# Retention attention and a gated MLP on one core: every engine in emission order, weights staged in buffers of later pairs, units between the attention pieces

## The chip, the core and the metric

The kernel runs on one core of a Trainium2 chip. A core has a matrix engine (TensorE, PE in the profile; PEld is its loading of weights), VectorE (DVE), ScalarE (ACT), GpSimd (POOL) and SyncE (SP), which only issues transfers here. Each engine takes its own instructions from its own queue in order; semaphores make one wait for another. TensorE writes to PSUM, a small accumulator memory of eight banks, from which VectorE and ScalarE read. Transfers between the off-chip memory and the on-chip SBUF run on 16 DMA engines and are issued from SyncE's, ScalarE's or GpSimd's queue. The metric is the device time of one execution in microseconds.

## The reference

Eight batches of 576 positions, eight heads of 64. The attention has no softmax: scores are scaled, multiplied by a decay that depends on the distance and on the head, and causal. Its result, with the heads side by side as 512 columns, is `x` of a gated MLP whose gate mixes positions within a batch.

```python
scores = scale * np.matmul(q, k.transpose(0, 1, 3, 2))
gamma = 1.0 - 2.0 ** (-5.0 - np.arange(H, dtype=np.float32))
Dmat = np.where(rel >= 0, gamma[:, None, None] ** rel[None, :, :], 0.0)
x = np.matmul(scores * Dmat, v)              # to (B, S, 512)
h = x @ w_in                                 # (.., 1024), then tanh-gelu
u, v = h[..., :512], h[..., 512:]
v_n = (v - mean(v)) / sqrt(var(v) + 1e-06) * g_ln
v_s = np.einsum('ts,bsd->btd', w_sg, v_n) + b_sg[None, :, None]
out = x + (u * v_s) @ w_out
```

Inputs and output are float32; the kernel computes its products in bfloat16.

## The kernel before

Two batches make a pair of 1152 positions, cut into nine tiles of 128 (NT = 9, MID = 4: tile 4 has the last 64 positions of one batch and the first 64 of the next). Four pairs make N = 36 tiles, numbered through. For tile i the pieces are:

- `load(i)`: q, k and v from memory, issued by SyncE, in runs of 64 floats; five buffers (pool `ld`).
- `prep(i)`, GpSimd: q and k to bfloat16 (`qkb`), v times the key's decay (`vsc`).
- `attn_T(i)`: eight transposes into `tp` (one PSUM buffer), copied to `qT` by VectorE and in two halves to `kbd` by ScalarE and VectorE. The three copies read one PSUM bank and are ordered one behind the other, as are the two of `zbd`.
- `attn_S(i)`: scores `sc`, masked by VectorE into `ret`. `attn_O(i)`: output `ot` from the running state `zbd` and from `ret`; VectorE multiplies by the decay table `ttab` into `xT`. `attn_Z(i)`: the state `zp`, copied in two halves to `zbd`.
- `mlp_V(i)`: product `hv`, gelu by ScalarE (`vg`), mean and variance by VectorE (`bst`, `mv`), three small steps of GpSimd (`rs`, `rs`, `nm`), and ScalarE's normalisation `vn`. `mlp_U(i)`: product `hu`, gelu into `uT`.

When a batch has all its `vn`, it gives units of work: four mixing units `mlp_W` (ten products `wp` with the transposed w_sg, `wT`, and two VectorE products into `gT`) and four or five output units `mlp_O` (eight products `op`, ScalarE's copy `ob`, and a store that ScalarE issues). Before, `release` and `flush` queue the units of a batch, and each turn of the main loop ends with two of them, `run(2)`. `hv`, `hu`, `wp` and `op` share three PSUM buffers (tag `d` of `psD`); a mixing unit takes two of them.

In front of the loop stand tables: masks, decays, rows of g_ln and b_sg (`build_rows`, `place_rows`), and the weights. w_in and w_out come through `ld` buffers that tile loads use too, and VectorE converts them; w_sg comes by GpSimd's converting transfers. `build_wT` makes `wT`, three pieces a turn from turn 3, through the buffer `tp` and VectorE.

TensorE, GpSimd and SyncE run in the order in which the code emits:

```python
    ctx.enter_context(tc.manual_schedule(engines={mybir.EngineType.PE, mybir.EngineType.Pool, mybir.EngineType.SP}))
```

VectorE's and ScalarE's instructions are ordered by a scheduler.

Of the kernel before, what the change touches and what calls it, by code (L numbers as in the profile page):

```python
# [11 lines left out]
F32 = mybir.dt.float32  # L12
# [7 lines left out]
def kernel(  # L20
# [24 lines left out]
    outf = out.rearrange("b s d -> (b s) d")  # L45

# [32 lines left out]
    row4 = consts.tile([4, 2, S], F32, name="row4")
    nc.scalar.dma_start(row4[:, 0, :F2], moe_g_ln.partition_broadcast(4))  # L80
    nc.scalar.dma_start(row4[:, 1, :], moe_b_sg.partition_broadcast(4))
    load(0)
    nc.scalar.dma_start(g_col[:], moe_g_ln.rearrange("(c p) -> p c", p=128))

# [4 lines left out]
    w_stage = []  # L89
    for half in (1, 0):  # L90
        for c in (0, 2):
            wst = ld.tile([128, 2, F2], F32, name="wst", tag="qk")
            nc.sync.dma_start(wst[:], moe_w_in.rearrange("(c p) f -> p c f", p=128)[:, c:c + 2, half * F2:(half + 1) * F2])
            w_stage.append((half, c, wst))
        load(1 if half else 2)

    def nonzero(ap, tmp):
        nc.vector.tensor_scalar(tmp, ap, 1e-20, None, op0=Alu.is_lt)  # L100
        nc.vector.scalar_tensor_tensor(tmp, ap, -1e-20, tmp, op0=Alu.is_gt, op1=Alu.mult)
        nc.vector.scalar_tensor_tensor(ap, tmp, 3e-20, ap, op0=Alu.mult, op1=Alu.add)

    g_tmp = consts.tile([128, KK], F32, name="g_tmp")
    nonzero(g_col[:], g_tmp[:])
    row4b = consts.tile([4, 2, S], BF, name="row4b")
    row_t = consts.tile([4, S], F32, name="row_t")
    sel_i = consts.tile([4, 1], I32, name="sel_i")
    nc.gpsimd.iota(sel_i[:], pattern=[[0, 1]], base=0, channel_multiplier=1)
    sel = consts.tile([4, 3], F32, name="sel")  # L110

    def build_rows():
        nonzero(row4[:, 0, :F2], row_t[:, :F2])
        nc.vector.reciprocal(row4[:, 0, :F2], row4[:, 0, :F2])
        nc.vector.tensor_copy(sel[:, 0:1], sel_i[:])
        nc.vector.tensor_scalar(sel[:, 1:2], sel[:, 0:1], 2.0, -1.0, op0=Alu.is_ge, op1=Alu.mult)
        nc.vector.scalar_tensor_tensor(sel[:, 2:3], sel[:, 1:2], -2.0, sel[:, 0:1], op0=Alu.mult, op1=Alu.subtract)
        for a, n in ((0, F2), (1, S)):
            nc.vector.tensor_copy(row4b[:, a, :n], row4[:, a, :n])
            nc.vector.scalar_tensor_tensor(row4b[:, a, :n], row4b[:, a, :n], sel[:, 1 + a:2 + a], row4[:, a, :n],  # L120
                                           op0=Alu.mult, op1=Alu.add)

    def place_rows():
        for t in vmid:
            nc.sync.dma_start(t[0][NB0:NB0 + 4, :], row4b[:, 0, :F2])
            nc.sync.dma_start(t[1][0:4, :], row4b[:, 0, :F2])
        nc.sync.dma_start(wT[0][SB - 1][NB0:NB0 + 4, :], row4b[:, 1, :])
        nc.sync.dma_start(wT[1][0][0:4, :], row4b[:, 1, :])

# [6 lines left out]
                            compare_op=Alu.is_ge, fill=0.0, base=0, channel_multiplier=-1)  # L136
    tri_mid = consts.tile([128, 128], BF, name="tri_mid")
    NB0 = S - 128 * MID
    nc.vector.tensor_copy(tri_mid[:], tri[:])
    nc.vector.memset(tri_mid[:NB0, NB0:], 0.0)  # L140

    pos_i = consts.tile([128, S], I32, name="pos_i")
    nc.gpsimd.iota(pos_i[:], pattern=[[1, S]], base=-ORG, channel_multiplier=0)
    pos_f = consts.tile([128, S], F32, name="pos_f")
    nc.vector.tensor_copy(pos_f[:], pos_i[:])
    srow_i = consts.tile([128, NT], I32, name="srow_i")
    nc.gpsimd.iota(srow_i[:], pattern=[[128, NT]], base=-ORG, channel_multiplier=1)
    srow = consts.tile([128, NT], F32, name="srow")
    nc.vector.tensor_copy(srow[:], srow_i[:])
    nc.vector.tensor_scalar(srow[:, MID + 1:], srow[:, MID + 1:], float(-S), None, op0=Alu.add)  # L150
    nc.vector.tensor_scalar(srow[NB0:, MID:MID + 1], srow[NB0:, MID:MID + 1], float(-S), None, op0=Alu.add)
# [4 lines left out]
    lg_col = consts.tile([128, KK], F32, name="lg_col")  # L156
    lsc = consts.tile([128, 1], F32, name="lsc")
    nc.vector.memset(lsc[:], math.log(1.0 / math.sqrt(D)))
    for h in range(H):
        nc.vector.memset(lg_col[(h % 2) * 64:(h % 2) * 64 + 64, h // 2:h // 2 + 1], lng[h])  # L160

    ttab = consts.tile([128, KK, 128 * SB], F32, name="ttab")

    def build_ttab():
        for kk in range(KK):
            nc.scalar.activation(ttab[:, kk, :S], pos_f[:], Act.Exp,
                                 scale=lg_col[:, kk:kk + 1], bias=lsc[:])
        nc.gpsimd.tensor_copy(ttab[:, :, S:], ttab[:, :, :128 * SB - S])

    mhalf = consts.tile([128, 1], F32, name="mhalf")  # L170
    nc.gpsimd.memset(mhalf[:], -0.5)

    NV, NK, NZ = 5, 2, 2
    vpads = [consts.tile([128, H * D], BF, name=f"vsc{i}") for i in range(NV)]
# [4 lines left out]
    vmid = [[consts.tile([128, F2], BF, name=f"vmid{i}{e}") for e in range(2)] for i in range(2)]  # L179
    for t in vmid:  # L180
        nc.gpsimd.memset(t[0][NB0:, :], 0.0)
        nc.gpsimd.memset(t[1][:NB0, :], 0.0)
    for t in kbds + zbds:
        nc.vector.memset(t[:], 0.0)
    nc.vector.memset(kmid[:NB0, :], 0.0)

    def load_wsg():
        nc.gpsimd.memset(wnat[:, :, 0:64], 0.0)
        nc.gpsimd.memset(wnat[:, :, 64 + S:], 0.0)
        for j in range(SB):  # L190
            n = min(128, S - 128 * j)
            nc.gpsimd.dma_start(wnat[:n, j, 64:64 + S], moe_w_sg[128 * j:128 * j + n, :])

    def load_wout():
        for c in (0, 2):
            wst = ld.tile([128, 2, F2], F32, name="wst", tag="qk")
            nc.sync.dma_start(wst[:], moe_w_out.rearrange("(c p) f -> p c f", p=128)[:, c:c + 2, :])
            for r in range(2):
                nc.vector.tensor_scalar(w_out[:, c + r, :], wst[:, r, :], g_col[:, c + r:c + r + 1], None, op0=Alu.mult)


    wT = [[consts.tile([128, S], BF, name=f"wT{e}_{j}") for j in range(SB)] for e in range(2)]

    def build_wT(e, j):
        c0 = (64 if e == 0 else 0) + 128 * j
        tp = psA.tile([128, S], BF, name="wtp", tag="tp")
# [3 lines left out]
        nc.vector.tensor_copy(wT[e][j][:], tp[:])  # L210
# [6 lines left out]
    def prep(i):  # L217
# [4 lines left out]
        vp = vpads[i % NV]  # L222
# [6 lines left out]
    def attn_T(i):  # L229
        s = st[i]  # L230
        tp = psA.tile([128, 2, KK, 128], BF, name="tp", tag="tp")
        for a in range(2):
            for kk in range(KK):
                nc.tensor.transpose(tp[:, a, kk, :], s["qkb"][:, a, kk * 128:(kk + 1) * 128], ident[:])  # L234
        qT = work.tile([128, KK, 128], BF, name="qT")
        nc.vector.tensor_copy(qT[:], tp[:, 0, :, :])  # L236
        kbd = kbds[i % NK]
        nc.scalar.activation(kbd[:64, :, 0, :], tp[:64, 1, :, :], Act.Copy)  # L238
        nc.vector.tensor_copy(kbd[64:, :, 1, :], tp[64:, 1, :, :])  # L239
        s["qT"], s["kbd"] = qT, kbd  # L240

    def attn_S(i):
        s = st[i]
        m = i % NT
        ret = work.tile([128, H, 128], BF, name="ret")
        msk = (tri_mid if m == MID else tri)
# [10 lines left out]
    def attn_O(i):  # L257
        s = st[i]
        p, m = divmod(i, NT)
        if m == 0:  # L260
            xTs[p] = pairp.tile([128, KK, NT * 128], BF, name="xT")
# [17 lines left out]
    def attn_Z(i):  # L279
        s = st[i]  # L280
        p, m = divmod(i, NT)
# [9 lines left out]
        zb = zbds[i % NZ]  # L291
        nc.vector.tensor_copy(zb[:64, :, 0:64], z[:64, :, 0:64])
        nc.scalar.activation(zb[64:, :, 64:], z[64:, :, 64:], Act.Copy)
# [3 lines left out]
    vns = {}  # L297

    def mlp_V(i):
# [6 lines left out]
        nc.scalar.activation(vg[:], hv[:], Act.Gelu_apprx_tanh)  # L306
        bst = work.tile([128, 6], F32, name="bst")
# [153 lines left out]
```

## Time and profile before

| | us |
|---|---|
| median of 3 runs | 276.59 |
| lowest, highest run | 276.05, 278.32 |
| profiled execution | 279.28 |
| its span, first to last instruction | 277.6 |

In the span TensorE is busy 226.5 us (82%), its weight loads 166.9 (60%), VectorE 184.9 (67%), ScalarE 130.3 (47%) and GpSimd 121.7 (44%). The transfers move 42.0 MB. These shares are averages over a start-up, a long middle and a short end that have different limits, so they name no bound by themselves. Matmuls are pipelined, so the distance from the start of one to the start of the next tells more than a duration. In lists in order of time a row has the start, the duration, the engine, the line, the operation, out<-in, shapes, a count, and in brackets how long the engine had been idle and what ended that.

### The profile page before, as it was taken

The numbers are of one execution on the slowest core, as the hardware profiler recorded it, in microseconds if no ns is written. First come the engines' busy times: TensorE is split into PE (matmuls) and PEld (weight loads), VectorE is DVE, ScalarE is ACT, GpSimd is POOL, SyncE is SP. The second block draws the span as 40 slices with busy tenths as digits, with TensorE's granted clock in tenths as the row PEclk, the third lists the DMA queues.
The fourth block names the chain that finished last, engine by engine and source line by source line (L and its number), as shares of the span: only waits on it lengthen the run. The fifth ranks groups of instructions, "written<-read, shape, count | busy, mean of one in ns | idle before, by whom it ended". The sixth has DMA issues, their size and how long they took to land.

```text
span 277.6 us, 6581 instructions
## 1 busy us (share of the span) xinstructions
PE 226.5 (82%) x2626; PEld 166.9 (60%) x2626; DVE 184.9 (67%) x400; ACT 130.3 (47%) x230; POOL 121.7 (44%) x208
## 2 busy tenths in 40 slices
PE   0138967767899789997999799969997999789894
PEld 0025745656676577665776676657675777566552
DVE  4996766645886687766866887657767876686230
ACT  1154514415344554664465445564454475544513
POOL 7069871243144465544444545446445444421100
PEclk9999989759999999999999999999999999999999
DMA  8999999599202899789958896765586022100315
GB/s 166 269 258 200 224 273 191 115 201 188 53 0 78 208 212 207 192 205 214 208 133 183 191 199 170 207 154 118 118 211 167 0 78 75 42 2 0 116 38 189
DMA packets 120606, 42.02 MB, mean 151 GB/s; under 512 B 113825, under 2 KB 114425, under 8 KB 120577
## 3 DMA queue, kind: packets, MB, share of 16 engines
q1 hardware_dynamic: 114192, 31.49, 54.3%
q10 hardware_dynamic: 5728, 9.46, 9.4%
q0 software_dynamic: 656, 0.66, 1.5%
q8 instruction: 20, 0.33, 0.5%
q14 instruction: 10, 0.07, 0.1%
HBM read 32.80 MB, written 9.44 MB: 152 GB/s over the span
## 4 chain that ended last, share of the span: by engine, by line
PE 40%; DVE 27%; ACT 12%; issue 7%; POOL 5%; DMA 4%; ACTq 3%; POOLq 0%; SPq 0%; DVEq 0%
PE wp L345 8%; PE hv L303 7%; PE hu L332 6%; DVE bst L308 5%; ACT vg L306 4%; DVE xT L276 4%; ACT ob L363 4%; PE op L357 4%; PE sc L251 4%; PE tp L234 3%; PE ot L268 2%; ACTq L364 2%; POOL rs L313 2%; DVE gT L350 2%; DVE kbd_169 L239 2%
## 5 line engine op out<-in xcount | busy, mean ns | idle before, releaser
L312 POOL TENSOR_SCALAR rs<-mv 128x1 f32<-128x1 f32 x36 | 8.0, 222 | 121.7 <-DVE mv L310 115.8
L253 DVE TENSOR_TENSOR ret<-sc,tri 128x512 bf16<-128x512 f32 x64 | 41.0, 681 | 10.9 <-PE sc L251 10.9
L322 ACT ACTIVATE vn<-vg,nm,rs 128x512 bf16<-128x512 f32 x32 | 26.0, 812 | 37.5 <-POOL nm L315 37.5
L332 PE MATMUL hu<-xT,w_in 128*128 128x128 bf16 x576 | 41.2, 229 | 0.6 <-ACT ob L363 0.6
L308 DVE BATCH_NORM_STATS2 bst<-vg 128x6 f32<-128x512 f32 x36 | 25.0, 694 | 23.3 <-ACT vg L306 22.7
L345 PEld LDWEIGHTS <-vn 128*128 128x128 bf16 x256 | 24.5, 97 | 25.4 <-issue 18.7
L306 ACT ACTIVATE vg<-hv 128x512 f32<-128x512 f32 x36 | 21.5, 597 | 37.3 <-PE hv L303 31.0
L303 PE MATMUL hv<-w_in,xT 128*128 128x512 bf16 x144 | 37.9, 387 | 1.3 <-DVE xT L276 1.3
L221 POOL CAST qkb<-qk 128x1024 bf16<-128x1024 f32 x36 | 37.7, 1046 | 0.9 <-DMA qk<-in_k_dram 0.8
L332 PEld LDWEIGHTS <-w_in 128*128 128x128 bf16 x576 | 36.8, 103 | 1.4 <-issue 0.8
L350 DVE TENSOR_TENSOR gT<-wp,uT 128x288 bf16<-128x288 f32 x64 | 26.1, 447 | 17.3 <-PE wp L345 17.3
L357 PE MATMUL op<-w_out,gT 128*128 128x512 bf16 x144 | 37.0, 379 | 0.0
L234 PE MATMUL tp<-ident,qkb 128*128 128x128 bf16 x288 | 24.1, 232 | 10.9 <-POOL qkb L221 7.8
L234 PEld LDWEIGHTS <-qkb 128*128 128x128 bf16 x288 | 20.6, 104 | 18.6 <-POOL qkb L221 8.1
L276 DVE TENSOR_TENSOR xT<-ot,ttab 128x512 bf16<-128x512 f32 x36 | 24.9, 690 | 6.6 <-PE ot L273 6.0
L363 ACT ACTIVATE ob<-op 128x512 f32<-128x512 f32 x36 | 21.4, 593 | 13.3 <-PE op L360 8.1
L335 ACT ACTIVATE uT<-hu 128x512 bf16<-128x512 f32 x36 | 21.2, 590 | 12.2 <-PE hu L332 12.2
L313 POOL TENSOR_TENSOR rs<-rs,mhalf 128x1 f32<-128x1 f32 x36 | 20.4, 567 | 3.0
L236 DVE COPY qT<-tp 128x512 bf16<-128x512 bf16 x36 | 15.0, 417 | 8.3 <-PE tp L234 8.1
L251 PE MATMUL sc<-qT,kbd_168 128*128 128x128 bf16 x144 | 11.6, 224 | 9.7 <-ACT kbd_168 L238 9.0
L303 PEld LDWEIGHTS <-xT 128*128 128x128 bf16 x144 | 12.6, 100 | 11.2 <-DVE xT L276 2.3
L357 PEld LDWEIGHTS <-gT 128*128 128x128 bf16 x144 | 12.5, 98 | 9.2 <-DVE gT L350 0.3
(130 smaller groups left out, 379.0 us busy)
## 6 DMA issues: line engine op xcount, KB each, us to landing
out_dram<-ob ACTq DMA_DIRECT2D x36, 256.0 KB, 2.0
qk<-in_q_dram SPq DMA_DIRECT2D x32, 256.0 KB, 3.9
qk<-in_k_dram SPq DMA_DIRECT2D x32, 256.0 KB, 4.9
vf<-in_v_dram SPq DMA_DIRECT2D x32, 256.0 KB, 4.7
wst<-in_moe_w_in_dram SPq DMA_DIRECT2D x4, 512.0 KB, 5.9
qk<-in_q_dram SPq DMA_DIRECT2D x8, 128.0 KB, 4.7
qk<-in_k_dram SPq DMA_DIRECT2D x8, 128.0 KB
vf<-in_v_dram SPq DMA_DIRECT2D x8, 128.0 KB, 4.3
```

The lines of the kernel that those rows point to most:

```text
L221: nc.gpsimd.tensor_copy(qkb[:], qk[:].rearrange("p a h d -> p a (h d)"))
L234: nc.tensor.transpose(tp[:, a, kk, :], s["qkb"][:, a, kk * 128:(kk + 1) * 128], ident[:])
L253: nc.vector.tensor_tensor(ret[:, 4 * j:4 * j + 4, :], sc[:], msk[:].unsqueeze(1).to_broadcast([128, 4, 128]), op=Alu.mult)
L276: nc.vector.tensor_tensor(xTs[p][:, :, 128 * m:128 * m + 128], ot[:], ttab[:, :, t0:t0 + 128], op=Alu.mult)
L303: nc.tensor.matmul(hv[:], xTs[p][:, kk, 128 * m:128 * m + 128], w_in[:, kk, F2:], start=(kk == 0), stop=(kk == KK - 1))
L306: nc.scalar.activation(vg[:], hv[:], Act.Gelu_apprx_tanh)
L308: nc.vector.bn_stats(bst[:], vg[:])
L332: nc.tensor.matmul(hu[:, c, :], w_in[:, kk, 128 * c:128 * c + 128], xTs[p][:, kk, 128 * m:128 * m + 128], start=(kk == 0), stop=(kk == KK ...
L345: nc.tensor.matmul(ps[half][:], vns[t0 + j][e][:, 128 * c:128 * c + 128], wT[e][j][:, half * HS:(half + 1) * HS], start=(j == 0), stop=(j ...
L350: nc.vector.tensor_tensor(gTs[p][:, c, col:col + HS], ps[half][:], uTs[p][:, c, col:col + HS], op=Alu.mult)
L357: nc.tensor.matmul(op[:], gTs[p][:, c, r], w_out[:, c, :], start=(c == 0), stop=False, skip_group_check=True)
L363: nc.scalar.activation(ob[:], op[:], Act.Copy)
```

## The change

- All five engines are put in emission order (`manual_schedule()` without a list, at the top of the kernel).
- The first tile is laid out by hand: tile 0's attention stands ahead of the tables that it doesn't need, tiles 1 and 2 are prepared between the conversions of w_in.
- Weights no longer use `ld` buffers. `stage` loads w_in, w_sg and w_out into buffers of `gT` and `uT` that later pairs use; SyncE issues all of them. ScalarE converts w_in and w_sg; VectorE scales w_out, at turn 4 ahead of that tile's masks.
- `wT` pieces go through `psD` buffers and ScalarE, one between two pieces of a turn, from turn 4.
- The rows of 1/g_ln are made from the column by four small transposes; VectorE places the rows by six copies in place of six transfers.
- `mlp_V` is split: `mlp_norm(i - 2)` opens a turn behind the scores, `mlp_stats` and `mlp_rstd` follow later. The units run one behind the scores and one behind the transposes. A batch's units are released at the start of the third turn after its last tile.
- In `attn_T` k is transposed ahead of q and ScalarE's half of `kbd` is copied first; in `attn_Z` ScalarE's half of `zbd` is first.

```diff
+    ctx.enter_context(tc.manual_schedule())
...
+    def stage(src, tag, shape):
+        st = pairp.tile(shape, F32, name="wst", tag=tag)
+        nc.sync.dma_start(st[:], src)
+        return st
+
+    load(0)
+    st_v = stage(w_in_r[:, :, F2:], "gT", [128, KK, F2])
+    load(1)
+    st_u = stage(w_in_r[:, :, :F2], "gT", [128, KK, F2])
...
+    def cast_w(dst, st):
+        for c in (0, 2):
+            nc.scalar.activation(dst[:, c:c + 2, :], st[:, c:c + 2, :], Act.Copy)
...
-        tp = psA.tile([128, S], BF, name="wtp", tag="tp")
+        tp = psD.tile([128, S], BF, name="wtp", tag="d")
...
-        nc.vector.tensor_copy(wT[e][j][:], tp[:])
+        nc.scalar.activation(wT[e][j][:], tp[:], Act.Copy)
...
-        for a in range(2):
+        for a in (1, 0):
...
-        nc.vector.tensor_copy(qT[:], tp[:, 0, :, :])
         kbd = kbds[i % NK]
         nc.scalar.activation(kbd[:64, :, 0, :], tp[:64, 1, :, :], Act.Copy)
+        nc.vector.tensor_copy(qT[:], tp[:, 0, :, :])
         nc.vector.tensor_copy(kbd[64:, :, 1, :], tp[64:, 1, :, :])
...
     prep(0)
     attn_T(0)
+    attn_S(0)
+    attn_O(0)
+    attn_Z(0)
+    late_tables()
+    build_rows()
+    cast_w(w_in[:, :, F2:], st_v)
+    load(2)
+    prep(1)
+    attn_T(1)
+    cast_w(w_in[:, :, :F2], st_u)
+    load(3)
+    prep(2)
+    load(4)
+    st_sg = load_wsg()
+    for i in range(1, N + 1):
+        if i >= 3 and (i - 3) in last:
+            wo += batch_work(last[i - 3])
         if i + 4 < N:
             load(i + 4)
+        if i == 1:
+            st_out = stage(w_out_r, "gT", [128, KK, DM])
         if i + 2 < N:
             prep(i + 2)
+        if i == 4:
+            for c in range(KK):
+                nc.vector.tensor_scalar(w_out[:, c, :], st_out[:, c, :], g_col[:, c:c + 1], None, op0=Alu.mult)
+        if i == 6:
+            place_rows()
         if i < N:
             attn_S(i)
+        if i >= 2:
+            mlp_norm(i - 2)
+        if i >= 4:
+            build_wT()
+        run()
+        mlp_V(i - 1)
+        if i >= 4:
+            build_wT()
         if i + 1 < N:
             attn_T(i + 1)
+        mlp_stats(i - 1)
+        if i >= 4:
+            build_wT()
+        run()
+        mlp_rstd(i - 1)
+        mlp_U(i - 1)
+        if i >= 4:
+            build_wT()
         if i < N:
             attn_O(i)
             attn_Z(i)
+        if i == 2:
+            build_rows2()
+        if i == 3:
+            cast_wsg(st_sg)
+    mlp_norm(N - 1)
+    run(len(wo))
+    wo += batch_work(B - 1)
+    run(len(wo))
```

What stands in the queues, at three places. ScalarE in a turn with two output units, before (from the gelu of `hv` to the next one; `ob` and its DMA are the copy and store of an output unit):

```order
L306 ACTIVATE vg<-hv 128x512
L238 ACTIVATE kbd_168<-tp 64x4x128
L335 ACTIVATE uT<-hu 128x4x128
L322 ACTIVATE vn<-vg,nm,rs 128x512
L293 ACTIVATE zbd_171<-zp 64x4x64
L363 ACTIVATE ob<-op 128x512
L364 DMA out_dram<-ob 128x512
L363 ACTIVATE ob<-op 128x512
L364 DMA out_dram<-ob 128x512
```

and after, the same turn from its normalisation on:

```order
L349 ACTIVATE vn<-vg,nm,rs 128x512
L390 ACTIVATE ob<-op 128x512
L391 DMA out_dram<-ob 128x512
L322 ACTIVATE vg<-hv 128x512
L254 ACTIVATE kbd_155<-tp 64x4x128
L390 ACTIVATE ob<-op 128x512
L391 DMA out_dram<-ob 128x512
L362 ACTIVATE uT<-hu 128x4x128
L308 ACTIVATE zbd_158<-zp 64x4x64
```

`vn`, now of the tile before, and one output copy with its DMA have moved ahead of `vg` and `kbd`. VectorE in a turn with two mixing units, before:

```order
L253 TENSOR_TENSOR ret<-sc,tri 128x512 x2
L308 BN_STATS bst<-vg 128x6
L236 COPY qT<-tp 128x512
L310 BN_AGGR mv<-bst 128x2
L276 TENSOR_TENSOR xT<-ot,ttab 128x4x128
L239 COPY kbd_168<-tp 64x4x128
L292 CAST zbd_171<-zp 64x4x64
L350 TENSOR_TENSOR gT<-wp,uT 128x288 x4
```

and after:

```order
L269 TENSOR_TENSOR ret<-sc,tri 128x512 x2
L377 TENSOR_TENSOR gT<-wp,uT 128x288 x2
L255 COPY qT<-tp 128x512
L256 COPY kbd_155<-tp 64x4x128
L327 BN_STATS bst<-vg 128x6
L377 TENSOR_TENSOR gT<-wp,uT 128x288 x2
L332 BN_AGGR mv<-bst 128x2
L292 TENSOR_TENSOR xT<-ot,ttab 128x4x128
L309 CAST zbd_158<-zp 64x4x64
```

The four `gT` products, which stood together at the end, are in two pairs; `bst` and `mv` now follow `qT` and `kbd` of the next tile. VectorE at the turn from tile 3 to tile 4, after the change (`w_out` is the scaling of the staged weight):

```order
L292 TENSOR_TENSOR xT<-ot,ttab 128x4x128
L309 CAST zbd_158<-zp 64x4x64
L436 TENSOR_SCALAR w_out<-wst,g_col 128x512 x4
L269 TENSOR_TENSOR ret<-sc,tri_mid 128x512 x2
L255 COPY qT<-tp 128x512
L256 COPY kbd_156<-tp 64x4x128
```

Before, the scaling stood a tile later, behind the masks of tile 5 and around `bst`; now it is ahead of the masks of tile 4.

245 lines of the change are left out of this document (110 added, 135 removed).

## The prediction

> **What bounds the kernel now.** I read the page first, then TensorE's order of time for the rhythm, then its waits and the DMA's stretches.
>
> ```profile
> span 277.6 us, 6581 instructions
> ...
> PE   0138967767899789997999799969997999789894
> ...
> PEclk9999989759999999999999999999999999999999
> ```
>
> There are two stages with different limits. In the first nine slices (62 us) TensorE is often idle and part of the time at half clock; from slice 11 on it is nearly full. Below, "tile i" begins with its score product (sc). The rows show the starts of tiles 7, 11, 12, 13, 14, 15 and 34, two mixing products (wp) that waited, and an output unit (op).
>
> ```profile
> 72.63 0.61 PE L251 MATMUL sc<-qT,kbd_169 128*128 128x128 bf16 x8
> ...
> 97.48 0.28 PE L345 MATMUL wp<-wT_0_191,vmid_174 128*128 128x288 bf16 x1 [1.43 <-DVE gT L350]
> ...
> 98.58 0.61 PE L251 MATMUL sc<-qT,kbd_169 128*128 128x128 bf16 x8
> ...
> 104.02 0.28 PE L345 MATMUL wp<-wT_0_191,vmid_174 128*128 128x288 bf16 x1 [0.38 <-DVE gT L350]
> ...
> 105.11 0.61 PE L251 MATMUL sc<-qT,kbd_168 128*128 128x128 bf16 x8
> ...
> 109.75 0.59 PE L357 MATMUL op<-w_out,gT 128*128 128x512 bf16 x2
> ...
> 110.83 0.61 PE L251 MATMUL sc<-qT,kbd_169 128*128 128x128 bf16 x8
> ...
> 116.46 0.61 PE L251 MATMUL sc<-qT,kbd_168 128*128 128x128 bf16 x8
> ...
> 121.09 0.65 PE L251 MATMUL sc<-qT,kbd_169 128*128 128x128 bf16 x8
> ...
> 244.93 0.61 PE L251 MATMUL sc<-qT,kbd_168 128*128 128x128 bf16 x8
> ```
>
> So there are three parts: 72.6 us up to tile 7; 244.93 - 72.63 = 172.3 us for the 27 tiles 7 to 33; 277.6 - 244.9 = 32.7 us to the end. In the middle a tile with two output units takes 5.63 us (110.83 to 116.46), one with a single unit 4.63 (116.46 to 121.09). An output unit is 1.08 us (109.75 to 110.83). A mixing unit is 10 products, of which nine take 98.58 - 97.48 = 1.10, so 1.22. A tile with two mixing units could thus take 5.63 + 2 x 0.14 = 5.9 us; tile 11 took 6.53, and its second unit waited:
>
> ```profile
> PE wp L345 <- DVE gT L350: 10.8, 12, 1.4
> ```
>
> (That row covers 72 to 245 us.) Two mixing units in a row need four of three PSUM buffers, so the second stands until VectorE has emptied the first. TensorE's floor for the six batches of units in tiles 7 to 33 (each two mixing and two output tiles, in three of them another tile with one unit): 6 x (2 x 5.9 + 2 x 5.6) + 3 x 4.6 = 152 us against 172.3. These 20 us are the most that another order of the same work can return there.
>
> **The change, part by part.** The sum is made against the profiled execution (279.28 us, span 277.6), 1.0% over the median of the runs (276.59); I scale at the end.
>
> *First tiles.* The columns that end the next three rows are granted clock, DMA share and GB/s.
>
> ```profile
> 0.00:20.00 20.00, 2.48 (x19) 1.77 (x20) 15.51 (x40) 5.82 (x14) 8.67 (x21) 1.00 0.99 232
> 20.00:40.00 20.00, 15.67 (x161) 11.32 (x160) 14.32 (x30) 7.76 (x13) 17.78 (x27) 0.99 1.17 224
> ...
> 102.00:108.00 6.00, 5.62 (x66) 4.38 (x67) 5.03 (x11) 2.32 (x6) 3.04 (x5) 1.00 1.01 220
> ...
> 5.64 1.04 POOL L221 CAST qkb<-qk 128x1024 bf16<-128x1024 f32 x1 [0.84 <-DMA qk<-in_k_dram]
> ...
> L166 ACT ACTIVATE ttab<-pos_f,lsc,lg_col 128x576 f32<-128x576 f32 x4 | 3.3, 857 | 9.5 <-DVE tri_mid L140 9.5
> ...
> L155 ACT ACTIVATE gv<-srow 128x9 f32<-128x9 f32 x8 | 0.9, 200 | 0.0
> ...
> 54.20 0.86 DVE L199 TENSOR_SCALAR w_out<-wst,g_col 128x512 bf16<-128x512 f32 x2
> ...
> 24.20 1.91 PE L303 MATMUL hv<-w_in,xT 128*128 128x512 bf16 x4
> ...
> 29.72 0.61 PE L251 MATMUL sc<-qT,kbd_168 128*128 128x128 bf16 x8
> ...
> 40.68 1.91 PE L332 MATMUL hu<-xT,w_in 128*128 128x128 bf16 x16
> ...
> 80.92 1.06 PE L332 MATMUL hu<-xT,w_in 128*128 128x128 bf16 x16
> ```
>
> When loads land: by 40 us the DMA has moved 20 us x (232 + 224) GB/s = 9.1 MB at full share. SyncE's new order has, up to the end of w_out, six tiles of 0.786 MB, w_in 2.1, w_sg 1.33 and w_out 1.05 MB, in all 9.2 MB, so w_out lands at about 40.4 us, and tiles 6, 7 and 8 0.786 MB / 0.215 = 3.7 us apart behind it (44, 48, 51.5). No entry of that queue waits for a buffer: w_out's needs ScalarE's first conversion of w_in, done by 16.
>
> The front gets quicker. Tile 0 is cast at 5.64 as before, then come transposes at half clock (1.0 us) and three copies of its PSUM buffer in series (0.58, 0.41, 0.43): its score product starts at 9.4, since the tables that took VectorE up to 15 us now stand behind it. Before tile 1, ScalarE converts half of w_in. No row shows such a conversion; from the ttab and gv rows 128x1024 is 0.2 + 1015 x (857 - 200)/567 ns = 1.4 us, with 0.86 (the shorter row) and 1.7 (twice it) as ends. From 12.9 two of them end at 15.7, the three copies at 17.1: tile 1. A tile without units is 5.63 - 2.16 = 3.5 us of products warm, up to twice that cold: tiles 2, 3, 4 at 23.5, 30 and 35. The second half of w_in is converted beside this, and if it weren't covered it would cost 2.8 us.
>
> Tile 4 stands: in VectorE's order the scaling of w_out is ahead of its masks (ret). They wait for 40.4 and four scalings (0.86 a pair), to 42.1, and end at 43.4. ScalarE converts w_sg meanwhile (five at 0.86, 35 to 39.4). TensorE, idle from 35.2 to 39.4, is at half clock then (hu x16 in 1.91 us at 40.68; 1.06 warm at 80.92), and wT, hv, wT, tp, wT, hu, wT and the output products last until 46.1. Tile 5 starts there. From its nm at 47 ScalarE has vn, wT, vg, wT and kbd (3.1 us, a wT taken as vg's 0.6), then VectorE two copies: tile 6 at 51. Tile 6 has two vmid of 0.81, wT, vg, wT and kbd from 53.3: tile 7 at **58** (before 72.6). Ends: 53, when only the landing of tile 7 (48) and its 5 us of cast, small steps and copies bind; 64, when DMA and chain each slip 3 us. The six rows that VectorE now copies, and their table, are some 3 us that lie under the waits for DMA; uncovered they would cost those 3 us.
>
> [...]
>
> *Middle.* The work of a tile stays the same; units move between the attention pieces, and the normalisation (vn) into the next tile's turn. With units apart the next hv and tp (1.3 us) cover VectorE's two gT products, so 5.9 us is reached where VectorE is on time. But the fixed order closes a ring through three engines, once per tile: ScalarE's vn, ob and its DMA issue, vg, kbd; VectorE's qT, kbd, bst, mv; GpSimd's three small steps; the next vn. qT now stands behind ScalarE's kbd, bst and mv behind qT. Before, bst and vn of a tile didn't wait for the next tile's copies. The ring's price from rows, start to start:
>
> ```profile
> 109.80 0.81 ACT L322 ACTIVATE vn<-vg,nm,rs 128x512 bf16<-128x512 f32 x1 [0.76 <-POOL nm L315]
> 110.52 0.58 ACT L363 ACTIVATE ob<-op 128x512 f32<-128x512 f32 x1
> ...
> 93.00 0.60 ACT L363 ACTIVATE ob<-op 128x512 f32<-128x512 f32 x1 [0.41 <-ACT ob L363]
> ...
> 94.02 0.60 ACT L306 ACTIVATE vg<-hv 128x512 f32<-128x512 f32 x1 [0.41 <-PE hu L332]
> 94.51 0.58 ACT L238 ACTIVATE kbd_169<-tp 64x512 bf16<-64x512 bf16 x1
> ...
> 107.86 0.41 DVE L236 COPY qT<-tp 128x512 bf16<-128x512 bf16 x1
> 108.19 0.17 DVE L310 BATCH_NORM_AGGREGATE mv<-bst 128x2 f32<-128x6 f32 x1
> ...
> 259.42 0.69 DVE L308 BATCH_NORM_STATS2 bst<-vg 128x6 f32<-128x512 f32 x1 [4.27 <-ACT vg L306]
> ...
> 260.22 0.18 DVE L310 BATCH_NORM_AGGREGATE mv<-bst 128x2 f32<-128x6 f32 x1
> ...
> 261.81 0.81 ACT L322 ACTIVATE vn<-vg,nm,rs 128x512 bf16<-128x512 f32 x1 [1.45 <-POOL nm L315]
> ```
>
> Output tile: vn to ob 0.72, ob to vg 1.02 (the DMA issue is in it), vg to kbd 0.49, kbd 0.58, qT 0.33, VectorE's kbd 0.40 (an estimate beside qT's pace), bst to mv 0.80, mv to vn 1.59: **5.93 us**, more than TensorE's 5.63. Mixing tile: no ob (less 1.02), bst's own 0.69 in place of 0.80, and two gT (0.82) ahead of mv: 5.6, less than TensorE's 5.9. So the ring binds output tiles once its slack is used up. After two mixing tiles vn starts 1.7 us into a tile (kbd ends at 3.8, qT, kbd, bst, gT until 6.0, 1.59, less 5.9). The next score product can't start before kbd is copied, 3.65 us after vn. The first output tile keeps 5.6 (vn slips to 2.0), the second takes 2.0 + 3.65 = 5.7, a third with one unit 5.9 to 6.0 in place of 4.6. Then vn is 2.3 us late and VectorE 1.8: unit one's gT end at 3.9 us in place of 2.7, unit two starts at 3.65 in place of 3.0, and this mixing tile takes 6.6, the next 5.9. Batches: 6.6 + 5.9 + 5.6 + 5.7 = 23.8, and 29.8 with the third output tile; three of each give **160.8 us** against 172.3. Ends: 152 with slack everywhere, 172 with nothing won.
>
> GpSimd's cast of tile i+2 is ahead of the small steps, so the DMA must be in time. A tile moves 0.786 in and 0.262 MB out: 4.8 us at 220 GB/s, under 5.9.
>
> *End.* The mixing of the batch before last now runs a tile later. From tile 34: 6.6 + 5.5 (no transposes) + 6.1 (hv, hu, four output units), then four mixing units, 1.22 + 3 x 1.68 (266.90 - 265.22), and the last outputs, 277.6 - 268.0 = 9.6, which don't change. Sum **34.1** against 32.7.
>
> ```profile
> 265.22 0.28 PE L345 MATMUL wp<-wT_0_191,vmid_176 128*128 128x288 bf16 x1 [0.30 <-DVE gT L350]
> ...
> 266.90 0.28 PE L345 MATMUL wp<-wT_0_191,vmid_176 128*128 128x288 bf16 x1 [0.30 <-DVE gT L350]
> ...
> 268.00 1.03 PE L357 MATMUL op<-w_out,gT 128*128 128x512 bf16 x4
> ...
> L364 ACTq DMA_DIRECT2D out_dram<-ob x36: 338/338/1042, 85.2 to 274.3; - x36
> ...
> DMA packets 120606, 42.02 MB, mean 151 GB/s; under 512 B 113825, under 2 KB 114425, under 8 KB 120577
> ```
>
> Span: 58.0 + 160.8 + 34.1 = 252.9, 24.7 less than before. Execution: 279.28 - 24.7 = 254.6; scaled by 276.59/279.28, **252 us**.
>
> **The rivals.** *The ring has slack and TensorE bounds the middle.* For: the same operations ran at 5.63 us a tile in another order, so no engine's own work is the bound. Against: the ring's rows follow each other by data or by queue and add to 5.93. The middle would be 152: 252.9 - 8.8 = 244.1, scaled 243.5; with tile 7 at 53, 238.5.
>
> *The middle wins nothing.* The ring at 6.4 us on each of 27 tiles makes 172.8; the front's 14.6 and the end's -1.4 remain: 264. For: a DMA issue of ScalarE has stood 1.04 us. Against: its median is 0.34.
>
> *Slower: loads arrive late.* GpSimd stands at the cast of tile i+2; the small steps, vn, kbd and the score product stand behind it. The gain is gone where a tile takes (160.8 + 24.7)/27 = 6.9 us, which is 1.05 MB at 152 GB/s; at 145 a tile takes 7.2 us and the kernel 286. Against: stretches at full share move 220 and more. The span's mean of 151 has idle DMA in it.
>
> That the change doesn't do what it says gets no chance: the built order has units apart and all engines as written.
>
> **How the numbers follow.** Forecast 0.74 (alone 245 to 260); ring with slack 0.12 (238 to 245); middle wins nothing 0.09 (260 to 272); late loads 0.05, of which 0.03 are slower and 0.02 about as before. Under 1% can't be told from no change (the runs spread by 0.8%). Faster by over 1%: 0.74 + 0.12 + 0.09 = 0.95; within 1%: 0.02; slower: 0.03. The range takes in parts of both neighbours: 242 to 264.
>
> **What would show it.** Tile 7's score product at 58; VectorE idle ahead of the scaling of w_out, ended by its DMA near 40; TensorE idle from about 35 to 39. In the middle, output tiles of 5.6 to 6.0 us, ScalarE's vn waiting for nm and VectorE's qT for ScalarE's kbd, a first mixing tile of 6.6. Wrong: 50 us for nine tiles (slack), a cast of GpSimd waiting for a load after 80 us (late loads), tile 7 past 64 (front).

## The result, and the profile after

The changed kernel takes 269.44 us (median of four runs, 266.47 to 270.21); the kernel before, on the same chip, took 276.75 (276.05 to 278.32). The ratio is 0.971, with a 95% interval of 0.962 to 0.979: faster by 3%, where 252 us was forecast and 242 to 264 given as the range. The profiled execution took 269.32 us. The head of the changed kernel's page:

```profile
span 267.6 us, 6555 instructions
...
PE   0558669868999999969999999799999999799894
...
PEclk9999986999999999999999999979999999889999
```

Over the first nine slices together TensorE is fuller than before. From there on it is full but for dents in slices 18, 26 and 35, and behind two of them, in slices 27 and 35 to 36, the granted clock dips. TensorE's order of time shows what stands there; these rows are starts of score products (sc) of tiles 7, 14, 15, 16, 25, 34 and 35, with the last products ahead of tile 16:

```profile
59.58 0.22 PE L267 MATMUL sc<-qT,kbd_156 128*128 128x128 bf16 x1
...
103.32 0.67 PE L267 MATMUL sc<-qT,kbd_155 128*128 128x128 bf16 x8
...
109.36 0.92 PE L267 MATMUL sc<-qT,kbd_156 128*128 128x128 bf16 x8
...
114.32 0.40 PE L305 MATMUL zp<-vsc_150,qkb 128*128 128x128 bf16 x4
116.36 0.22 PE L267 MATMUL sc<-qT,kbd_155 128*128 128x128 bf16 x1 [1.64 <-ACT uT L362]
...
173.16 0.22 PE L267 MATMUL sc<-qT,kbd_156 128*128 128x128 bf16 x1 [1.64 <-ACT uT L362]
...
231.09 0.22 PE L267 MATMUL sc<-qT,kbd_155 128*128 128x128 bf16 x1 [1.63 <-ACT uT L362]
...
239.49 0.61 PE L267 MATMUL sc<-qT,kbd_156 128*128 128x128 bf16 x8
```

- Front: tile 7 at 59.6 us, forecast 58.0, before 72.6. The gain is there.
- Middle, tiles 7 to 33: 231.09 - 59.58 = **171.5** us, forecast 160.8, before 172.3. Nothing is gained.
- End: 267.6 - 231.1 = 36.5, forecast 34.1, before 32.7.

So 10.7 of the 14.7 us by which the span of 252.9 was missed lie in the middle. There the output tile from 103.32 takes 6.04, and the one with a single unit 7.00 (109.36 to 116.36), in which TensorE stands for 1.64 us ahead of tile 16's score product. The row names uT of ScalarE, which is only the last semaphore seen; the engines' own order (below) shows qT written just then. The waits of the middle, grouped (waiting engine and line, what ended the wait, us in total, times, longest):

```profile
ACT vn L349 <- POOL nm L337: 35.3, 24, 2.5
DVE qT L255 <- ACT kbd_155 L254: 24.5, 14, 3.0
DVE qT L255 <- ACT kbd_156 L254: 20.8, 13, 3.0
...
PE sc L267 <- ACT uT L362: 4.9, 3, 1.6
```

ScalarE waits for GpSimd's nm ahead of every vn (24 times, and three more ahead of a vmid), VectorE for ScalarE's kbd ahead of every qT (27 of 27). That is the ring of the forecast. Its links, from the vn in tile 14's turn to the normalisations of the next two turns (ScalarE, VectorE and GpSimd in order of time):

```profile
105.82 0.82 ACT L349 ACTIVATE vn<-vg,nm,rs 128x512 bf16<-128x512 f32 x1 [1.46 <-POOL nm L337]
106.66 0.60 ACT L390 ACTIVATE ob<-op 128x512 f32<-128x512 f32 x1
107.28 0.34 ACTq L391 DMA_DIRECT2D out_dram<-ob  x1
107.67 0.60 ACT L322 ACTIVATE vg<-hv 128x512 f32<-128x512 f32 x1 [0.41 <-ACT ob L390]
108.16 0.58 ACT L254 ACTIVATE kbd_156<-tp 64x512 bf16<-64x512 bf16 x1
108.77 0.42 DVE L255 COPY qT<-tp 128x512 bf16<-128x512 bf16 x1 [2.15 <-ACT kbd_156 L254]
109.23 0.43 DVE L256 COPY kbd_156<-tp 64x512 bf16<-64x512 bf16 x1
109.69 0.69 DVE L327 BATCH_NORM_STATS2 bst<-vg 128x6 f32<-128x512 f32 x1
110.49 0.18 DVE L332 BATCH_NORM_AGGREGATE mv<-bst 128x2 f32<-128x6 f32 x1
112.10 0.81 ACT L346 ACTIVATE vmid_162<-vg,nm,rs 64x512 bf16<-64x512 f32 x1 [1.46 <-POOL nm L337]
112.93 0.81 ACT L346 ACTIVATE vmid_163<-vg,nm,rs 64x512 bf16<-64x512 f32 x1
113.76 0.60 ACT L390 ACTIVATE ob<-op 128x512 f32<-128x512 f32 x1
...
115.27 0.58 ACT L254 ACTIVATE kbd_155<-tp 64x512 bf16<-64x512 bf16 x1
...
115.88 0.42 DVE L255 COPY qT<-tp 128x512 bf16<-128x512 bf16 x1 [2.97 <-ACT kbd_155 L254]
...
119.21 0.81 ACT L349 ACTIVATE vn<-vg,nm,rs 128x512 bf16<-128x512 f32 x1 [2.48 <-POOL nm L337]
```

Start to start it is 0.84 (vn to ob), 1.01, 0.49, 0.61, 0.46, 0.46, 0.80 and 1.61: 6.28 us from 105.82 to 112.10, against 5.93 in the forecast. The next round takes 7.11 (to 119.21), because the tile over the batch border is normalised in two vmid of 0.83 each, and this falls in the very turn with a single output unit (15, 24 and 33). In that turn ScalarE's kbd ends at 115.85, qT at 116.30, and TensorE, done with zp at 114.72, stands until 116.36.

### The profile page after: what moved, and what is told of

The parts are those of the page before. It is cut to its first block, busy times and chain, and to the rows that moved or that the text cites. A ratio compares the mean times of both kernels' runs of the same rounds, so it can differ in the third digit from the quotient of the medians.

```text
span 267.6 us, 6555 instructions
## 1 busy us (share of the span) xinstructions
PE 227.5 (85%) x2594; PEld 164.6 (62%) x2630; DVE 176.4 (66%) x394; ACT 143.1 (53%) x249; POOL 117.6 (44%) x202
## 4 chain that ended last, share of the span: by engine, by line
PE 40%; DVE 19%; SPq 12%; ACT 10%; issue 8%; DMA 4%; POOL 4%; ACTq 2%; POOLq 0%; DVEq 0%
PE wp L372 13%; SPq L78 10%; PE hv L319 7%; PE hu L359 6%; DMA qk<-in_k_dram 4%; DVE bst L327 4%; DVE xT L292 3%; PE op L384 3%; ACT ob L390 3%; PE tp L251 3%; DVE qT L255 3%; DVE gT L377 3%; PE ot L284 2%; ACT kbd_155 L254 2%; ACT kbd_156 L254 2%
## 5 line engine op out<-in xcount | busy, mean ns | idle before, releaser
L255 DVE COPY qT<-tp 128x512 bf16<-128x512 bf16 x36 | 15.2, 424 | 60.0 <-ACT kbd_155 L254 35.3
L238 POOL CAST qkb<-qk 128x1024 bf16<-128x1024 f32 x36 | 37.4, 1038 | 21.3 <-DMA qk<-in_k_dram 17.1
L359 PE MATMUL hu<-xT,w_in 128*128 128x128 bf16 x576 | 39.4, 224 | 1.5 <-ACT wT_3_186 L227 1.5
L359 PEld LDWEIGHTS <-w_in 128*128 128x128 bf16 x576 | 35.5, 100 | 2.4 <-issue 1.6
L384 PE MATMUL op<-w_out,gT 128*128 128x512 bf16 x128 | 34.7, 379 | 0.8
L267 PE MATMUL sc<-qT,kbd_156 128*128 128x128 bf16 x144 | 13.0, 225 | 5.7 <-ACT uT L362 2.4
```

The source lines that it names most:

```text
L238: nc.gpsimd.tensor_copy(qkb[:], qk[:].rearrange("p a h d -> p a (h d)"))
L359: nc.tensor.matmul(hu[:, c, :], w_in[:, kk, 128 * c:128 * c + 128], xTs[p][:, kk, 128 * m:128 * m + 128], start=(kk == 0), stop=(kk == KK ...
L384: nc.tensor.matmul(op[:], gTs[p][:, c, r], w_out[:, c, :], start=(c == 0), stop=False, skip_group_check=True)
```

## The experiments

The theory: **the closed ring through ScalarE, VectorE and GpSimd sets the middle.** Against it stand: the loads, VectorE's own queue, and ScalarE's load as such (its work, not the closing of a loop). Each ratio below is to the kernel before, run on the same chip in the same session (medians of 278.4 to 279.6 us); the changed kernel's is 0.971 (0.962 to 0.979).

**Open the ring at vn.**

```diff
         attn_S(i)
-        if i >= 2:
-            mlp_norm(i - 2)
...
             attn_T(i + 1)
+        if i >= 2:
+            mlp_norm(i - 2)
```

> ScalarE's normalisation (vn) of tile i-2 is emitted behind the copies of tile i+1's transposes, and so behind kbd, in place of ahead of the first unit. Everything else is the changed kernel. Ring theory (vn, ob, vg, kbd, qT, kbd, bst, mv, vn, 6.29 us per output tile in the changed kernel, sets the middle): vn no longer delays kbd, the loop is open, TensorE bounds the tiles: mixing 5.9, output 5.6, one-unit output about 4.6 to 5; the four waits of a first score product (1.6 us each) and the two half-clock stretches behind them go. Tiles 7 to 33 take 152 to 157 us in place of 171.5, the kernel 249 to 255 in place of 269. Rival 'loads': the DMA sets the pace, and the time stays within 2 us of 269. Rival 'VectorE': its queue (gT twice, ret, xT in a fixed order) sets the mixing tiles: those stay at 7.2, only the output tiles shorten, 263 or more.

Measured: 249.6 us, ratio 0.894 (0.886 to 0.901). The middle took 157.1 us (59.94 to 217.01) in the profiled execution, which was the longest of the four (253.3 us). TensorE's score products of tiles 15 and 16, and ScalarE around one vn:

```profile
108.50 0.61 PE L267 MATMUL sc<-qT,kbd 128*128 128x128 bf16 x8
...
113.13 0.72 PE L267 MATMUL sc<-qT,kbd 128*128 128x128 bf16 x8
```

```profile
106.02 0.58 ACT L254 ACTIVATE kbd<-tp 64x512 bf16<-64x512 bf16 x1
106.49 0.81 ACT L349 ACTIVATE vn<-vg,nm,rs 128x512 bf16<-128x512 f32 x1
```

The one-unit tile takes 4.63 in place of 7.00 and has no wait; vn starts with no wait of its own, behind kbd. No instruction was added or taken away, so neither the loads nor ScalarE's or VectorE's work can be what the changed kernel's middle stood for.

**Open it at another link.**

```diff
         mlp_V(i - 1)
+        mlp_stats(i - 1)
+        mlp_rstd(i - 1)
...
-        mlp_stats(i - 1)
...
-        mlp_rstd(i - 1)
```

> VectorE's bst and mv of tile i-1, and GpSimd's three steps behind them, are emitted right behind hv, ahead of tile i+1's transposes and copies; vn stays ahead of vg and kbd. Ring theory: the loop is now vn, ob, vg, bst, mv, vn: 0.84 + 1.01 + 0.6 + 0.8 + 1.62 = 4.9 us, less than TensorE's 5.6, and no longer goes through kbd and qT; qT and the next score product stand 0.5 us later behind vg than before, which the slack takes. Middle 153 to 159, kernel 250 to 257: about as much as with vn moved. If instead it is only vn's place ahead of kbd that counts (ScalarE's load, not a closed loop), this edit gives nothing or loses: 268 to 272.

Measured: 249.3 us, ratio 0.894 (0.887 to 0.902), the middle 156.0 us (56.97 to 212.99). VectorE's order, with mv ahead of the copies:

```profile
107.67 0.69 DVE L327 BATCH_NORM_STATS2 bst<-vg 128x6 f32<-128x512 f32 x1 [1.74 <-ACT vg L322]
108.47 0.18 DVE L332 BATCH_NORM_AGGREGATE mv<-bst 128x2 f32<-128x6 f32 x1
108.57 0.39 DVE L255 COPY qT<-tp 128x512 bf16<-128x512 bf16 x1
108.99 0.43 DVE L256 COPY kbd<-tp 64x512 bf16<-64x512 bf16 x1
```

Here vn stays ahead of kbd and the gain is the same. The loop that is left (vn, ob, vg, bst, mv, vn) is shorter than TensorE's tile by the estimate above, 4.9 against 5.6 us. Two edits at different engines, each of which takes links out of the ring, return 14.4 and 15.5 us of the middle: it is the closed loop, and not the place of vn.

**Shorten one link.** The stores go to SyncE's queue.

```diff
-        nc.scalar.dma_start(outf[128 * i:128 * i + 128, :], ob[:])
+        nc.sync.dma_start(outf[128 * i:128 * i + 128, :], ob[:])
```

> The stores of output rows are issued by SyncE, not by ScalarE; each load of SyncE's queue then stands behind the stores written ahead of it. Ring theory: ob to vg falls from 1.01 to about 0.65, the ring of an output tile from 6.29 to 5.9; some 13 output tiles of the middle shorten by up to 0.4 and the start of the mixing behind them by the same, in all 4 to 6 us: 263 to 266. Rival 'loads': loads are delayed behind stores that wait for ob, and the kernel is slower than 269, by 2 us or more.

Measured: 257.0 us, ratio 0.922 (0.915 to 0.930), more than expected. The middle took 162.0 us (57.84 to 219.86). ScalarE, two rounds of the ring:

```profile
96.68 0.81 ACT L349 ACTIVATE vn<-vg,nm,rs 128x512 bf16<-128x512 f32 x1 [1.25 <-POOL nm L337]
97.52 0.60 ACT L390 ACTIVATE ob<-op 128x512 f32<-128x512 f32 x1
98.02 0.59 ACT L322 ACTIVATE vg<-hv 128x512 f32<-128x512 f32 x1
...
102.44 0.81 ACT L349 ACTIVATE vn<-vg,nm,rs 128x512 bf16<-128x512 f32 x1 [1.39 <-POOL nm L337]
```

ob to vg fell from 1.01 to 0.50, and the round from 6.28 to 5.76. That is about what TensorE needs for a second output tile (5.72 in this run, and the same with the ring open), so lateness no longer builds up from one output tile to the next, which the expectation had left out: the second output tiles and the one-unit tiles of the middle sum to 34.3 and 17.2 us, near the 34.2 and 18.0 of the forecast. The first mixing tiles still sum to 41.8 in place of 39.6. So the middle is 1.2 us over the forecast although the ring is 0.17 us shorter than the 5.93 priced there: the forecast's price of lateness in a first mixing tile (6.6 us) was too low as well. Stores ahead of loads did not make the kernel slower.

**Take only the second vmid out of the ring.** `mlp_norm` gets a list of the halves that it does; the second half of the border tile is done behind `attn_T(i + 1)`.

```diff
-            mlp_norm(i - 2)
+            mlp_norm(i - 2, (0,))
...
             attn_T(i + 1)
+        if i >= 2:
+            mlp_norm(i - 2, (1,))
```

> Only the second of the two vmid activations of a tile over the batch border (0.81 us each) moves behind kbd; all other tiles keep vn where it is. Ring theory: in the three turns that have it (15, 24, 33) the ring is 0.83 shorter, the one-unit output tile takes 6.2 in place of 7.05, the middle is 2.5 us shorter; the first score product behind it waits 0.8 in place of 1.64, and if that saves the two stretches at half clock, 2.4 more. 264 to 267 in place of 269. Rival 'loads' or 'VectorE': no change, 268 to 270, since ScalarE is not what these turns wait for.

Measured: 262.7 us, ratio 0.943 (0.935 to 0.950), and 167.7 for the middle. TensorE at tiles 15 and 16:

```profile
107.75 0.92 PE L267 MATMUL sc<-qT,kbd 128*128 128x128 bf16 x8
...
113.93 0.22 PE L267 MATMUL sc<-qT,kbd 128*128 128x128 bf16 x1 [0.82 <-DVE qT L255]
```

The one-unit tile takes 6.18 and the wait 0.82, as expected. Behind the wait TensorE kept its pace (at tile 25 two mixing products took 0.41 us, in the changed kernel 0.69), the granted clock of the whole profiled execution was 0.987 against 0.973, and the kernel gains a little more than the expected 264 to 267 us.

**The front: w_out scaled later, then also loaded later.** The forecast had tile 4 stand for w_out.

```diff
-        if i == 4:
+        if i == 7:
             for c in range(KK):
                 nc.vector.tensor_scalar(w_out[:, c, :], st_out[:, c, :], g_col[:, c:c + 1], None, op0=Alu.mult)
```

> The scaling of w_out by VectorE is emitted in turn 7 in place of turn 4; its load stays where it is in SyncE's queue. The middle is untouched. Theory 'w_out stands in VectorE's queue': tile 4's masks (ret) no longer wait 3.2 us for the load of w_out and 1.7 us behind it; tile 5 starts at 42 to 43 in place of 46.2, tile 7 at 56 to 57 in place of 59.6, the kernel 265 to 267. Rival 'loads set the front': GpSimd's cast of tile 6 stands for its load until about 43 whatever VectorE does (it waited 5.8 us there), so tiles 6 and 7 come as late as before: tile 7 at 59 to 60, 268 to 270.

Measured: 273.4 us, 0.977 (0.966 to 0.987): no gain. Tile 4 still took 9.8 us (36.99 to 46.78) and tile 7 came at 58.94. But tile 7 itself took 11.0 (to 69.97): the four scalings, 2.52 us in one piece, now stand between its mixing units.

```diff
-        if i == 1:
+        if i == 4:
             st_out = stage(w_out_r, "gT", [128, KK, DM])
...
-        if i == 4:
+        if i == 8:
             for c in range(KK):
```

> The load of w_out (1.05 MB) moves in SyncE's queue from ahead of tile 6 to behind tile 8, and the scaling to turn 8. Theory 'loads set the front': tiles 6, 7 and 8 land some 4.6 us earlier (1.05 MB at 228 GB/s), tile 7 starts at 54 to 56 in place of 59.6, the kernel 263 to 266. Theory 'only VectorE's queue': tile 7 at 56 to 57, no better than with the scaling alone moved. If w_out then lands too late for its first output unit at tile 9, tiles 8 and 9 show it.

Measured: 270.8 us, 0.971 (0.963 to 0.979). Tile 4 took 9.5 us (36.18 to 45.70), tile 7 came at 57.80, tile 8 took 7.7. Neither theory held: without the wait for w_out something else held tile 4. The changed kernel's own rows name it. TensorE, ScalarE, VectorE and GpSimd in tile 4:

```profile
36.49 2.40 ACT L212 ACTIVATE wnat<-wst 128x576 bf16<-128x576 f32 x4
37.23 0.23 PE L226 MATMUL wtp<-ident,wnat 128*128 128x128 bf16 x1 [0.45 <-ACT wnat L212]
...
39.52 0.23 PE L226 MATMUL wtp<-ident,wnat 64*128 64x64 bf16 x1 [0.28 <-ACT wnat L213]
...
41.32 1.67 DVE L436 TENSOR_SCALAR w_out<-wst,g_col 128x512 bf16<-128x512 f32 x4 [3.17 <-DMA wst<-in_moe_w_out_dram]
...
45.04 1.04 POOL L238 CAST qkb<-qk 128x1024 bf16<-128x1024 f32 x1 [5.82 <-DMA qk<-in_k_dram]
```

TensorE's first transposes of w_sg (wtp) stand for ScalarE's conversion of it (wnat), one piece at a time, until 39.5; VectorE stands 3.17 us for w_out, until 41.32; GpSimd stands 5.82 us for the load of tile 6, until 45.04. Three waits lie beside each other, and from within the first of them on TensorE is at half clock (granted clock 0.50 from 37.9 to 44.7 us). Two of the waits taken away together, w_out as in the last edit and, at all four places of `build_wT`:

```diff
-        if i >= 4:
+        if i >= 5:
             build_wT()
```

> w_out loaded behind tile 8 and scaled in turn 8, and the transposes of w_sg begin in turn 5 in place of turn 4, so that in turn 4 TensorE waits neither for masks behind w_out nor for ScalarE's conversion of w_sg. If these two, each hidden by the other, hold tile 4 (10.3 us in the changed kernel, 9.5 with w_out alone moved), tile 4 takes 6 to 7 us and tile 7 starts at 54 to 56; tiles 5 to 7 take up to 2 us more each for the work moved there; the kernel 265 to 269. If the loads of tiles 6 and 7 hold it whatever TensorE does, tile 7 stays at 57 to 60.

Measured: 268.1 us, 0.960 (0.952 to 0.968). Tile 4 fell to 7.5 us (36.20 to 43.72) and tile 7 came at 56.65, short of the expected 54 to 56; the moved work came back in tiles 7 and 8 (8.5 and 7.7 us), and tile 9 began at 72.80, in the changed kernel at 72.70. Nothing is left of it.

**The front: is it the early first tile?** First the tables of VectorE (`late_tables`, `build_rows`) were put back ahead of `prep(0)`.

> VectorE's late tables and the small rows stand ahead of tile 0's copies again, as they did before the change; all else is the changed kernel. Tile 0's score product moves from 9.2 to about 16.8, since the tables wait for ScalarE's ttab until 15. If the front is a chain from tile 0 on, tile 7 comes 5 to 7.6 us later (65 to 67) and the kernel takes 274 to 277: the early start of tile 0 is most of the front's gain. If loads and w_out set it from tile 4 on (w_out lands at about 39), the delay is taken up in the idle time of tiles 2 to 4: tile 7 at 60 to 62, the kernel 269 to 272.

Measured: 267.9 us, 0.960 (0.951 to 0.969). The premise was wrong: tile 0 moved only from 9.18 to 9.74. What had kept it until 16.8 before the change is in the trace of before: ScalarE's kbd waited for VectorE's qT, and qT stood in VectorE's queue behind a reciprocal over 4 x 512 values and further steps on rows of that size.

```profile
9.09 3.34 DVE L114 RECIPROCAL row_80<-row_80 4x512 f32<-4x512 f32 x1
...
15.72 0.40 DVE L236 COPY qT<-tp 128x512 bf16<-128x512 bf16 x1
...
16.16 0.59 ACT L238 ACTIVATE kbd_168<-tp 64x512 bf16<-64x512 bf16 x1 [0.86 <-DVE qT L236]
```

In the changed kernel the rows are made from four columns and the reciprocal takes 0.18, so these tables are short wherever they stand. So tile 0 was delayed by force:

```diff
+    hold = consts.tile([4, F2], F32, name="hold")
+    nc.vector.memset(hold[:], 1.0)
+    for _ in range(2):
+        nc.vector.reciprocal(hold[:], hold[:])
     srow = consts.tile([128, NT], F32, name="srow")
```

> Two reciprocals over 4 rows of 512 (3.34 us each in the trace of before) are put into VectorE's queue ahead of the row numbers from which ScalarE makes its tables. They compute nothing that is used; all else is the changed kernel. Tile 0's score product moves from 9.2 to about 16, where it stood before the change. If the front is a chain from tile 0 on, tile 7 comes 6 to 7 us later (65 to 67) and the kernel takes 274 to 277: the early tile 0 is half of the front's gain. If the loads set the front (GpSimd's casts waited 17 us for them), the delay is taken up by tile 4 and tile 7 starts at 59 to 62, the kernel 268 to 272: the front's gain then comes from the order of the loads and the work of tiles 1 to 6, not from tile 0.

Measured: 271.9 us, 0.978 (0.970 to 0.987), no difference from the changed kernel that these runs can tell. TensorE's score products of tiles 0 and 7:

```profile
14.36 0.26 PE L271 MATMUL sc<-qT,kbd 128*128 128x128 bf16 x1 [6.38 <-DVE qT L259]
...
59.91 0.22 PE L271 MATMUL sc<-qT,kbd 128*128 128x128 bf16 x1
```

Tile 0 came 5.2 us later and tile 7 only 0.3. The early first tile is not what the front gains by.

**Put together,** from the edits above and no others. vn late, statistics first, w_out loaded and scaled late:

> The three edits together: vn behind kbd, bst and mv ahead of qT, w_out loaded and scaled late. The ring is open at two places. If each of the two alone opens it, together they bring little more in the middle (154 to 157 us, against 157.1 and 156.0), and the front's gain adds: tile 7 at 53 to 55, the kernel 243 to 247. If something else holds the middle at 156 (the mixing tiles with 6.0 and 6.4 us), the middle does not fall under 155.

Measured: 250.6 us, 0.896 (0.887 to 0.906), over the expected 243 to 247: the middle 157.8, tile 7 at 55.41, but tile 8 took 7.7 us, since w_out's scaling stands there. Without the edit of w_out:

> vn behind kbd, and bst and mv ahead of qT; w_out as in the changed kernel. The ring is open at two places. Either alone gave a middle of 157.1 and 156.0. If TensorE bounds it then, together they give 155 to 157 and 247 to 251; if each left a different remainder of the ring, 152 to 154 and 244 to 247.

Measured: 248.8 us, 0.892 (0.886 to 0.897), the middle 155.9. And the statistics first with the stores on SyncE:

> bst and mv ahead of qT, and the stores issued by SyncE. With the ring open there is no wait left that ScalarE's 0.5 us per store would shorten: middle 155 to 157, 247 to 251, the same as with bst and mv moved alone (249.3). If stores ahead of loads hold loads back, over 251.

Measured: **246.9 us**, 0.886 (0.881 to 0.890), the middle 154.4 (57.06 to 211.46): the lowest median of all, though its interval overlaps those of the other four kernels with an open ring. All kernels with an open ring take 154 to 158 us in the middle, near the 152 that was TensorE's floor in the forecast.

## Why the prediction was wrong

Point by point, in the order of its steps.

- **First tiles: right in the number, half right in the reason.** Tiles 4, 5, 6 and 7 were forecast at 35, 46.1, 51 and 58 and came at 35.9, 46.2, 52.7 and 59.6. TensorE stood for the conversion of w_sg until 39.5 (forecast 39.4) and worked at half clock behind it, as forecast. How long, which the 46.1 rests on, was the author's estimate, from the 5.5 us between hv at 24.20 and sc at 29.72 in the trace of before; hv took 1.91 us there and 1.03 later, but the granted clock reads 1.00 over those 5.5 us, so no half clock is shown there. In the changed kernel's tile 4 it was 0.50 from 37.9 to 44.7 us. VectorE's wait for w_out was there too, but taking it away brought tile 7 only 1.8 us forward and tile 9 not at all. Before, the tables did hold VectorE until 15.7, but that tile 0 is early because they now stand behind it was wrong: they may stand ahead of it, since they have become short, and a late tile 0 costs 0.3 us at tile 7. Which part of the change returned the front's 13 us is not settled; three of the candidates alone (w_out's place, the tables' place, tile 0) are excluded by runs. A fourth stands in the trace of before and was not tested. At tile 3 the changed kernel is 4.0 us ahead (29.80 against 33.75), so 9 of the 13 us come between tiles 3 and 7. In that stretch TensorE stood 9.9 us, in ten waits, for VectorE's copies of wT, which went through the buffer `tp` of the attention's own transposes. Two of the ten (29.7 to 72.6 us):

```profile
PE wtp L209 <- DVE wT_1_192 L210: 2.4, 1, 2.4
...
PE wtp L209 <- DVE wT_3_189 L210: 1.4, 1, 1.4
```

  After the change, with these copies on ScalarE and in other buffers, TensorE waits 2.5 us for them up to tile 7.
- **Middle: the step that failed is the ring's price,** "5.93 us", and with it the one-unit output tile of "5.9 to 6.0" and the first mixing tile of 6.6. By kind of tile, from the 28 starts of tiles 7 to 34:

| tiles (count) | forecast, us | measured, us | difference |
|---|---|---|---|
| first mixing (6) | 39.6 | 44.9 | +5.3 |
| second mixing (6) | 35.4 | 35.3 | -0.1 |
| first output (6) | 33.6 | 33.4 | -0.2 |
| second output (6) | 34.2 | 36.9 | +2.7 |
| one-unit output (3) | 18.0 | 21.1 | +3.1 |
| sum | 160.8 | 171.5 | +10.7 |

  The four links that were mis-sized: vn to ob 0.84 (forecast 0.72), kbd's end to qT 0.03 (0), qT to kbd of VectorE 0.46 (0.33), kbd to bst 0.46 (0.40). With mv to vn (1.61 for 1.59) and ob to vg (1.01 for 1.02) they are 0.35 us a round. That doubled the excess over TensorE's 5.63 from 0.30 to 0.65 per output tile. The second vmid, 0.83 in the turns with one output unit, was not in the sum at all, though the same two vmid had been counted for tile 6 in the front. Half of the excess is paid in the first mixing tiles, where the forecast had 6.6 and 7.2 to 8.5 came (8.5 once, with half clock). Taking the second vmid out of the ring returned 3.8 us of the middle; shortening one link by 0.5 brought it to 162.0, and opening the ring to 156 to 157.
- **The rival that came nearest** is "the middle wins nothing" (260 to 272 us), with the ring at 6.4 us on each of 27 tiles. Its outcome is right, its reason only in part. The ring is 6.28 on an output tile and 7.11 three times, but the second mixing and the first output tiles, 12 of the 27, took what the forecast had. A store issue of 1.04 us, which spoke for that rival, did not come: after the change ScalarE's longest is 0.41. The rival of late loads fell: the casts of GpSimd waited for loads 17.1 us in all, none of it after 46 us. The rival of slack had no ring that binds; only the kernels that open it, at 247 to 251 us, come near its times (238 to 245).
- **End: 36.5 against 34.1.** Its first tile, 34, took 8.40 in place of 6.6, which is again the ring, with half clock (granted clock 0.50 from 232.5 to 235.8 us). With the ring open the end took 34.1 to 34.7 us.
- **Before and after take the same 172 us in the middle for different reasons.** Before, the second of two adjoining mixing units waited for VectorE, 10.8 us in the middle. That wait has fallen to 1.2 us, and the ring has taken its place: the two totals agree within 0.8 us, which is chance.

## What to carry to other kernels

When a fixed order replaces a scheduler, follow each engine's queue once around the loop: a chain that leaves an engine and comes back to it in the next turn is a lower bound on the turn. Here it was opened without added work, by moving one emission behind what it needn't precede. Price such a ring from starts, not from durations, leave a margin on each link (even the pair vn to ob took 0.72 us in one trace and 0.84 in the other), and look for the turn in which a special tile adds to it. Here the forecast ring was 5% over TensorE's time, and 0.03 to 0.13 us on four links doubled that. And before crediting a start-up's gain to the first thing that got earlier, delay that thing on purpose.

## What the runs showed of the hardware

**Behind a wait of 1.6 us TensorE slowed down in 12 places of 18.** In the changed kernel TensorE stood for 1.64 us ahead of tile 25, made one product, stood for another 0.24 and went on at 173.62; from 174.4 to 177.8 us the granted clock was 0.50. The stretch by windows (the columns that end a row are the granted clock, DMA share and GB/s):

```profile
167.00:174.00 7.00, 4.99 (x65) 3.43 (x64) 3.83 (x9) 4.57 (x9) 3.05 (x5) 1.00 0.76 190
174.00:178.00 4.00, 3.78 (x21) 2.16 (x20) 3.40 (x8) 0.82 (x2) 3.04 (x5) 0.57 0.70 108
178.00:187.00 9.00, 8.71 (x115) 7.13 (x114) 6.82 (x15) 3.97 (x8) 3.04 (x5) 1.00 0.67 137
```

This happened at tiles 25 and 34 and not at tile 16, whose wait was the same; the first mixing tile behind it took 8.49 and 8.40 us against 7.35, so it cost 1.1 us. The same wait (1.63 to 1.71 us) stands at these three tiles in the five kernels that change only the front. Over the six kernels two mixing products behind it took 0.68 or 0.69 us (as at tiles 25 and 34 above) at 12 of the 18 waits and 0.41 (as at tile 16) at the other six. In the seven kernels where the wait is 0.94 us or less (the second vmid taken out, the stores moved, the ring open) the products behind it kept their pace at all the places that the rows show, 20 of 21. What decides between the 12 and the six no run here shows.

**A store issued by ScalarE cost that engine 0.5 us, not its 0.34.** The issue row has 0.34 us, but ob to the next gelu went from 1.01 to 0.50 us when SyncE issued the store.

**The distance to the next start was not fixed by an instruction's own time.** VectorE's qT, with 0.41 to 0.42 us of its own (0.39 in the run with the statistics ahead), is followed by mv after 0.33 us in the trace of before and by kbd after 0.46 in the trace after, but after 0.42 with the statistics ahead of the copies. ScalarE's vn is followed by ob after 0.72 us in the middle of before, and after 0.84 in most turns of the changed kernel (0.72 in three). What decides it no run here shows.
